# One load of wo split by rows: 96 rows in one DMA, 32 rows in four DMAs of eight

## The chip, the core and the metric

The kernel runs on one core of one Trainium2 chip. A core has TensorE (PE, matrix multiplies), VectorE (DVE), ScalarE (ACT), GpSimd (POOL) and SyncE (SP), which work side by side and wait for one another through semaphores. Data comes from the large memory (HBM) into the on-chip memory of 128 partitions, one row of a tile in each, by 16 DMA engines. A DMA instruction is issued on an engine's queue, here nearly always SP's; its rows are dealt to DMA engines, each of which moves its share packet by packet and then adds to the DMA's semaphore. The load counts as landed when the last of them has done so.

The metric is the device time of one execution in microseconds (us).

## The reference

One decode step of a gated mix of two layers, all in bf16, for four batches of one token with 512 features. Cut to what matters:

```python
# A: attention over the last 4096 of 16384 cached positions
q = (x @ wq)                      # 512 -> 32 heads of 128
k, v = last 4096 rows of the caches, 8 kv heads, each for 4 query heads
p = softmax(q k^T * 128 ** -0.5)
a = (p v) @ wo                    # 4096 -> 512
# B: gated linear unit
b = (relu(x @ W_gate) * (x @ W_up)) @ W_down     # 512 -> 1792 -> 512
g = sigmoid(sum(x * gate_w))
out = g * a + (1 - g) * b
```

The caches make up 64 of the 81 MB that are read; wo is 4 MB (4096 x 512).

## The kernel before

**Sets.** The work on the caches is cut into eight sets (NSET): one batch and four of the eight kv heads each. A set loads 4 MB of keys (`load_k`, L158) and 4 MB of values (`load_v`, L162), each as one DMA of 128 rows of 32 KB, into two buffers used in turn. PE turns the keys over (`kt`, L249), ACT and DVE copy them back, PE makes the scores (`scores`), DVE and ACT the softmax (`maximum`, `exponent`, `turn`), PE the product with the values (`values`, L328), and `combine` (L345) puts the heads' outputs, divided by their sums and weighted by g, into the tile oq.

**Order of the work.** The program is written out by hand. `Program` holds a list per engine, in the order in which `P.op` and `P.dma` are called; names stand for semaphore values, and an instruction waits for the names it lists. Every DMA has a semaphore of its own. `emit` (L59) writes one wait instruction for each semaphore that is needed and not yet seen by that engine.

**Loads.** All large loads go through SP's queue in one order: keys 0, wq, then keys and values by turns, W_gate and W_up (into the buffer that keys 6 have left), values 7, W_down, and last wo. SP waits before an issue only for the buffer to be free. wo goes into Wbig, where wq was, and so waits for Q, the last use of wq, which has long passed by then.

**wo.** Partition p of Wbig holds rows 32p to 32p + 31 of wo one behind another, 32 x 512 numbers, 32 KB. The load is cut by these 32 blocks at `WO_CUTS = (0, 16, 28, 32)` into three DMAs of all 128 partitions, with 16, 12 and 4 KB in each partition (L181 to L183). Sixteen DMA engines have eight partitions each.

**The end.** The last values and `combine(7)` are followed by W_down's 56 matmuls (L444), which start the sum in a PSUM bank AB, and wo's 128 (L452), four for each of the 32 blocks, which add to it. A wo matmul uses all 128 partitions of its block, so the 64 of the first piece can begin only when every row of it has landed:

```python
        for k in range(len(WO_CUTS) - 1):
            for i in range(WO_CUTS[k], WO_CUTS[k + 1]):
                ...
                        ("ACC",) if last else None, [("WO", k), ("OQ", NSET - 1)])
```

Then DVE copies AB (L456), PE turns it over (L459), DVE copies it again (L460) and SP stores it (L461).

Of the kernel before, what the change touches and what calls it, by code (L numbers as in the profile page):

```python
# [19 lines left out]
NSET = 8  # L20
# [9 lines left out]
WO_CUTS = (0, 16, 28, 32)  # L30
# [49 lines left out]
def bass_gated_mix__sliding_block_cached__glu_gated_reglu__decode_kernel(  # L80
# [13 lines left out]
    with ExitStack() as ctx:  # L94
        def sb(name, shape, dt):
            return ctx.enter_context(nc.sbuf_tensor(name, shape, dt))
# [3 lines left out]
        Wbig = sb("Wbig", [128, 16384], BF16)  # L100
# [47 lines left out]
        P = Program()  # L148
# [29 lines left out]
        P.dma("sp", lambda e: e.dma_start(Vsb[:, 0, 0:NFT * 512], B_W_down.rearrange("(p i) w -> p (i w)", p=128)),  # L178
              ("WD",), [("PV", NSET - 2, 3)])
        wo_src = A_wo.rearrange("(p i) w -> p (i w)", p=128)  # L180
        for k in range(len(WO_CUTS) - 1):  # L181
            lo, hi = 512 * WO_CUTS[k], 512 * WO_CUTS[k + 1]
            P.dma("sp", lambda e, lo=lo, hi=hi: e.dma_start(Wbig[:, lo:hi], wo_src[:, lo:hi]), ("WO", k), [("Q",)])  # L183


        P.op("pool", lambda e: e.memset(ones[:, :], 1.0), ("ONES",))
# [261 lines left out]
        for k in range(len(WO_CUTS) - 1):  # L448
            for i in range(WO_CUTS[k], WO_CUTS[k + 1]):
                for cb in range(4):  # L450
                    last = i == 31 and cb == 3
                    P.op("pe", lambda e, i=i, cb=cb, last=last: e.matmul(  # L452
                        AB[:, 4 * cb:4 * cb + 4], Wo3[:, i, cb * 128:(cb + 1) * 128], oq3[:, :, i],
                        start=False, stop=last, skip_group_check=True),
                        ("ACC",) if last else None, [("WO", k), ("OQ", NSET - 1)])
        P.op("dve", lambda e: e.tensor_copy(outT[:, :].rearrange("p (b c) -> p c b", c=4),  # L456
                                            AB[:, 0:16].rearrange("p (c b) -> p c b", c=4)), ("OUTT",), [("ACC",)])
        otb = SCB[1][:].bitcast(BF16)
# [54 lines left out]
```

## Time and profile before

| | |
|---|---|
| median of three runs | 199.39 us (199.17 to 199.5) |
| the profiled execution's own time | 199.14 us |
| its span, first to last instruction | 197.4 us |
| mean granted TensorE clock | 0.843 |
| read from HBM | 81.01 MB, 410 GB/s over the span |
| wo's three loads: issued at | 168.31, 168.75 and about 169.2 us |
| wo's three loads: time from issue to landing | 20.9, 24.1 and 24.9 us |
| W_down's matmuls (L444) | from 188.02, 1.65 us |
| wo's matmuls (L452) | from 189.53, 1.85 us, and from 192.94, 1.87 us |
| the output's store issued (L461) | 195.65 us |

The profile is one execution on the chip. Times are in us from the start of the span. The page gives busy time by engine, then slices of the span, DMA queues, the chain of work that ended last, and the costliest groups of instructions; in such a group the form is line, engine, operation, result <- operands, how often, and at the end the idle time before it with what ended it. Loads are listed with their size in KB and the median time from issue to landing. "SPq" is SP's own instruction stream, where the DMAs are issued.

### The profile page before, as it was taken

Reading aid. Unit: us, or ns where it says so; the run is one execution under the profiler, and the core shown is the slowest. Engines: PE = TensorE matmul, PEld = TensorE weight load, DVE = VectorE, ACT = ScalarE, POOL = GpSimd, SP = SyncE. Lnnn points to the kernel's source line nnn. Section 1 sums busy time; section 2 is a strip of 40 time slices with the busy share of each in tenths; the row PEclk is TensorE's granted clock in tenths of the full one; section 3 lists DMA queues with packets and bytes.
Section 4 is the critical chain, followed back from the end, with each engine's and each line's share of the span. In section 5 each row is a group of like instructions: output and inputs, shape, how many; then the busy total and the mean of one; then the engine's idle time right before and its main releaser. Section 6 shows DMA issues by size and latency. Waiting matters only on the chain.

```text
span 197.4 us, 4201 instructions
## 1 busy us (share of the span) xinstructions
PE 144.9 (73%) x1859; PEld 111.4 (56%) x1859; DVE 102.5 (52%) x277; ACT 91.6 (46%) x108; POOL 6.3 (3%) x31
## 2 busy tenths in 40 slices
PE   0139975989399929993999498839981999259874
PEld 0038842956287527753875386438641875259673
DVE  0105428395559457844684578437843694641110
ACT  2008800896097419740965198318830974400000
POOL 7500000000000000000000000000000000000000
PEclk9999965599979996997599789987999799955555
DMA  5999999999999999999999999999999999999970
GB/s 213 425 425 432 432 461 468 418 438 420 422 425 425 422 425 427 422 438 428 432 451 428 418 451 430 432 425 422 432 428 425 425 395 433 449 424 406 432 332 30
DMA packets 3371, 81.27 MB, mean 412 GB/s; under 512 B 405, under 2 KB 410, under 8 KB 538
## 3 DMA queue, kind: packets, MB, share of 16 engines
q1 hardware_dynamic: 3344, 81.01, 95.9%
q8 instruction: 14, 0.23, 0.5%
q14 instruction: 3, 0.02, 0.0%
q10 hardware_dynamic: 10, 0.01, 0.0%
HBM read 81.01 MB, written 0.00 MB: 410 GB/s over the span
## 4 chain that ended last, share of the span: by engine, by line
DMA 64%; PE 21%; ACT 6%; DVE 5%; SPq 1%; issue 1%
DMA Ksb<-in_A_k_cache_dram 52%; PE bank L260 13%; DMA Wbig<-in_A_wo_dram 12%; ACT Ksb L265 5%; PE bank L281 4%; DVE Ksb L267 3%; PE bank L337 2%; ACT sc L318 2%; DVE pT L325 1%; PE bank L350 1%; PE bank L452 1%; DVE sc L289 1%; SPq L159 0%; SPq L169 0%; SPq L183 0%
## 5 line engine op out<-in xcount | busy, mean ns | idle before, releaser
L260 PE MATMUL bank<-identf,Ksb 128*128 128x128 f32 x512 | 82.8, 319 | 32.1 <-DMA Ksb<-in_A_k_cache_dram 29.3
L265 ACT ACTIVATE Ksb<-bank 128x1024 bf16<-128x1024 bf16 x72 | 71.0, 1023 | 70.8 <-PE bank L260 70.5
L260 PEld LDWEIGHTS bank<-identf,Ksb 128*128 128x128 f32 x512 | 68.4, 164 | 46.8 <-DMA Ksb<-in_A_k_cache_dram 32.0
L267 DVE COPY Ksb<-bank 128x1024 bf16<-128x1024 bf16 x56 | 38.2, 686 | 47.4 <-PE bank L260 46.3
L289 DVE CUSTOM_DVE_ANT_0 sc<-bank,mask 128x512 bf16<-128x512 f32 x32 | 22.0, 687 | 11.3 <-PE bank L281 11.1
L281 PE MATMUL bank<-Ksb,QS 128*32 128x512 bf16 x256 | 21.2, 420 | 3.0 <-DVE Ksb L267 1.6
L325 DVE STREAM_TRANSPOSE pT<-sc 128x1024 bf16<-128x1024 bf16 x16 | 19.7, 1237 | 2.9 <-ACT sc L318 2.8
L337 PE MATMUL bank<-Vsb,pT 128*32 128x256 bf16 x512 | 20.8, 291 | 0.0
L318 ACT ACTIVATE sc<-sc,negmax 128x1024 bf16<-128x1024 bf16 x16 | 18.3, 1144 | 4.8 <-DVE negmax L310 4.7
L337 PEld LDWEIGHTS bank<-Vsb,pT 128*32 128x32 bf16 x512 | 12.8, 101 | 6.5 <-issue 2.4
L350 PEld LDWEIGHTS bank<-osb,Wsel 128*64 128x64 f32 x128 | 8.8, 148 | 4.6 <-issue 2.6
L281 PEld LDWEIGHTS bank<-Ksb,QS 128*32 128x32 bf16 x256 | 4.5, 100 | 11.3 <-DVE Ksb L267 4.1
L385 PE MATMUL bank<-xT,Ksb 128*128 128x4 bf16 x112 | 6.9, 199 | 5.3 <-DVE oq L358 5.3
L350 PE MATMUL bank<-osb,Wsel 128*64 128x32 f32 x128 | 9.7, 233 | 1.2 <-DVE mq L296 0.7
L385 PEld LDWEIGHTS bank<-xT,Ksb 128*128 128x128 bf16 x112 | 6.8, 162 | 5.3 <-issue 5.3
L310 DVE TENSOR_SCALAR negmax<-mall 32x1 f32<-32x1 f32 x32 | 4.6, 144 | 1.0
L296 DVE TENSOR_REDUCE mq<-mx 32x1 f32<-32x4 f32 x32 | 4.6, 143 | 0.8
L452 PE MATMUL bank<-oq,Wbig 128*128 128x4 bf16 x128 | 3.7, 168 | 1.6 <-DMA Wbig<-in_A_wo_dram 1.6
L342 DVE COPY osb<-bank 128x256 f32<-128x256 f32 x8 | 3.4, 420 | 2.8 <-PE bank L337 2.8
L227 PE MATMUL bank<-ident,xsb 5*128 5x5 bf16 x4 | 0.3, 167 | 5.8 <-POOL m L203 5.8
L452 PEld LDWEIGHTS bank<-oq,Wbig 128*128 128x128 bf16 x128 | 3.6, 103 | 1.6 <-DMA Wbig<-in_A_wo_dram 1.6
L389 DVE TENSOR_SCALAR gtmp<-bank 128x56 f32<-128x56 f32 x1 | 0.2, 217 | 7.0 <-PE bank L385 7.0
(55 smaller groups left out, 44.9 us busy)
## 6 DMA issues: line engine op xcount, KB each, us to landing
Ksb<-in_A_k_cache_dram SPq DMA_DIRECT2D x8, 4096.0 KB, 23.1
Vsb<-in_A_v_cache_dram SPq DMA_DIRECT2D x8, 4096.0 KB, 32.5
Wbig<-in_A_wq_dram SPq DMA_DIRECT2D x1, 4096.0 KB, 21.4
Wbig<-in_A_wo_dram SPq DMA_DIRECT2D x1, 2048.0 KB, 20.9
Ksb<-in_B_W_gate_dram SPq DMA_DIRECT2D x1, 1792.0 KB, 19.0
Ksb<-in_B_W_up_dram SPq DMA_DIRECT2D x1, 1792.0 KB, 22.9
Vsb<-in_B_W_down_dram SPq DMA_DIRECT2D x1, 1792.0 KB, 16.4
Wbig<-in_A_wo_dram SPq DMA_DIRECT2D x1, 1536.0 KB, 24.1
```

The costliest lines, as they stand in the source:

```text
L260: P.op("pe", lambda e, bk=bk, cc=cc, c=c, s=s: e.transpose(bk[:, cc * 128:(cc + 1) * 128], kw[:, c * 128:(c + 1) * 128], identf[:, :]), (" ...
L265: P.op("act", lambda e: e.activation(dst, bk[:, :].bitcast(BF16), ACTF.Copy), ("KTC", s, i), [("KT", s, i)])
L267: P.op("dve", lambda e: e.tensor_copy(dst, bk[:, :].bitcast(BF16)), ("KTC", s, i), [("KT", s, i)])
L281: P.op("pe", lambda e, a=a, h=h: e.matmul(bk[32 * a:32 * a + 32, 0:512], QS[:, NSET * h + s, :], k4[:, 16 * bank:16 * bank + 16, 32 * a:32 ...
L289: P.op("dve", lambda e: e.tensor_tensor_reduce(sc[:, s % 2, bank * 512:(bank + 1) * 512], bk[:, :], mask[:, :], 1.0, LOWEST, ALU.add, ALU.max,
L296: P.op("dve", lambda e, a=a: e.tensor_reduce(mq[:, a:a + 1], mx[32 * a:32 * a + 32, par, :], AXIS.X, ALU.max), ("MAXQ", s, a), [("SCC", s, ...
L318: P.op("act", lambda e: e.activation(sc[:, par, k * PW:(k + 1) * PW], sc[:, par, k * PW:(k + 1) * PW], ACTF.Exp, bias=negmax[:, par:par + ...
L325: P.op("dve", lambda e: e.transpose(pT[:, par, k * PW:(k + 1) * PW], sc[:, par, k * PW:(k + 1) * PW]), ("PTT", s, k), [("EXP", s, k), ("PV ...
L337: P.op("pe", lambda e, c=c, g=g, col=col: e.matmul(OB[32 * g:32 * g + 32, 0:256], pT[:, par, col:col + 32], v3[:, 16 * k + c, :], start=(k ...
L350: P.op("pe", lambda e, k=k, lo=lo: e.matmul(FB[r, 256:288], Wsel[:, lo:lo + 64], osb[:, par, 32 * k:32 * k + 32], start=(k == 0), stop=(k ...
L385: P.op("pe", lambda e, W=W, i=i, t=t, col=col: e.matmul(FB[:, col:col + 4], W[:, t, i:i + NFT * 127 + 1:NFT], xT[:, t * 8:t * 8 + 4], star ...
L452: P.op("pe", lambda e, i=i, cb=cb, last=last: e.matmul(AB[:, 4 * cb:4 * cb + 4], Wo3[:, i, cb * 128:(cb + 1) * 128], oq3[:, :, i], start=F ...
```

## The change

The first of wo's three loads is issued as five DMAs in place of one: rows 0 to 95 in one DMA, and rows 96 to 127 in four of eight rows each. The columns (16 KB in each partition) stay as they are, and so do the second and third loads, so that wo takes seven DMAs instead of three. The matmuls of the first piece wait for the five semaphores of its parts. No other instruction is changed; SP has four DMA instructions more, PE four waits more.

```diff
         wo_src = A_wo.rearrange("(p i) w -> p (i w)", p=128)
-        for k in range(len(WO_CUTS) - 1):
+        def load_wo(k, r0, r1):
             lo, hi = 512 * WO_CUTS[k], 512 * WO_CUTS[k + 1]
-            P.dma("sp", lambda e, lo=lo, hi=hi: e.dma_start(Wbig[:, lo:hi], wo_src[:, lo:hi]), ("WO", k), [("Q",)])
+            P.dma("sp", lambda e: e.dma_start(Wbig[r0:r1, lo:hi], wo_src[r0:r1, lo:hi]), ("WO", k, r0), [("Q",)])
+
+        load_wo(0, 0, 96)
+        for r0 in range(96, 128, 8):
+            load_wo(0, r0, r0 + 8)
+        for k in range(1, len(WO_CUTS) - 1):
+            load_wo(k, 0, 128)
+        wo_parts = [[("WO", 0, r0) for r0 in (0, 96, 104, 112, 120)]] + [[("WO", k, 0)] for k in range(1, len(WO_CUTS) - 1)]
...
                         start=False, stop=last, skip_group_check=True),
-                        ("ACC",) if last else None, [("WO", k), ("OQ", NSET - 1)])
+                        ("ACC",) if last else None, wo_parts[k] + [("OQ", NSET - 1)])
```

## The prediction

> **What bounds the kernel now.** I read the page first: engine shares, DMA line and queues.
>
> ```profile
> PE 144.9 (73%) x1859; PEld 111.4 (56%) x1859; DVE 102.5 (52%) x277; ACT 91.6 (46%) x108; POOL 6.3 (3%) x31
> ...
> DMA  5999999999999999999999999999999999999970
> ...
> q1 hardware_dynamic: 3344, 81.01, 95.9%
> q8 instruction: 14, 0.23, 0.5%
> q14 instruction: 3, 0.02, 0.0%
> ```
>
> No compute engine is full; the DMA engines are, from the second slice to the 38th. SP's queue (q1) moves 81.01 MB and fills 95.9% of the time of 16 engines. The kernel is as long as its loads, so what matters is how evenly the last ones end. Note also the 14 small packets of q8 (16 KB each) and the three of q14 (8 KB): they fetch instructions and use the same engines.
>
> Then the chain that ended last, at its end, and the timeline of the same stretch:
>
> ```profile
> 168.31 0.43 SPq L183
> 168.75 0.04 issue
> 168.79 24.11 DMA Wbig<-in_A_wo_dram
> 192.89 0.04 issue
> 192.94 1.88 PE bank L452 x64
> 194.85 0.21 DVE outT L456
> ```
>
> ```profile
> 189.53 1.85 PE L452 MATMUL bank<-oq,Wbig 128*128 128x4 bf16 x64
> 192.94 1.87 PE L452 MATMUL bank<-oq,Wbig 128*128 128x4 bf16 x64 [1.56 <-DMA Wbig<-in_A_wo_dram]
> ```
>
> PE uses wo's first piece from 189.53 to 191.38, idles 1.56 us, and goes on when the second piece has landed, at 192.89. From there to the end of the span is 4.5 us of dependent work. The first piece (landed 189.2) does not hold PE: at 189.53 PE had just finished w_down. The third (194.2) is in before PE comes to it, 48 matmuls after 192.94, at about 194.35. So the time to watch is the landing of the second piece on its slowest engine. Sizes and landings:
>
> ```profile
> Wbig<-in_A_wo_dram SPq DMA_DIRECT2D x1, 2048.0 KB, 20.9
> Vsb<-in_B_W_down_dram SPq DMA_DIRECT2D x1, 1792.0 KB, 16.4
> Wbig<-in_A_wo_dram SPq DMA_DIRECT2D x1, 1536.0 KB, 24.1
> Wbig<-in_A_wo_dram SPq DMA_DIRECT2D x1, 512.0 KB, 24.9
> xsb<-in_A_x_dram ACTq DMA_DIRECT2D x1, 4.0 KB
> ```
>
> Last, the trace's records of single DMA packets (start, length, size, queue; not the engine). On one engine a packet starts about 4 ns before the one ahead ends, so 16 chains can be followed through, and each ends its share of a load with a 4-byte semaphore packet. These 16 per load show the skew. For the second piece (clock of the span): six engines at 189.66 to 189.95, one at 190.46, one at 191.81, three at 191.16 to 191.42, and five at 192.82 to 192.90. The cause is in the chains. Each q8 fetch costs its engine about 1.55 us (1.0 to 1.1 us itself, 0.5 us more on the next packet) and the 14 go round the same eight engines: five had two before the end, three had one. The other eight have none; on one of them two q14 fetches fell (0.94 + 0.99 us: the one at 191.81), on another one (0.68: at 190.46). So there is a slow eight, ending at 192.90, and a fast eight, ending at 191.81 with seven of them by 190.46.
>
> **The change, part by part.** *Removed:* one load of 128 rows of 16 KB; each engine had eight rows of 611 ns: 4.89 us. *Added:* a load of 96 rows, six an engine (3.67 us), and four loads of eight rows. x's load of four rows left four semaphore packets, four engines with one row each; so I take eight rows as eight engines with a row each, the same eight every time. Those get 6 + 4 = 10 rows, the other eight 6. If a row costs 611 ns wherever it goes, the ten-row engines end 1.22 us later, the six-row engines 1.22 us earlier. Each of four further semaphore packets takes 6 ns: 0.02. Thus +1.25 and -1.22.
>
> *Which eight.* The trace does not number its engines. gate_w's load (one row, one engine) sat in a chain without q8 fetches, by its place among the 32 KB packets, though another chain lies 3 ns off. [...] I take them to be the fast eight.
>
> *What a row costs when eight neighbouring rows are written at once.* This decides, and the trace has no large case. Below: 0.61 us a load of eight rows, the price of one row by itself. Above: 4.89 us, since in every large load here one engine alone fills its eight rows and no such set was filled faster. Between lies the only load in which several engines write neighbouring rows: x's. Its four packets of 1 KB took 93, 51, 44 and 44 ns and 92 ns from first start to last end: 4 KB in 92 ns, 44.5 GB/s for four engines, where one 16 KB packet alone runs at 16384/611 = 26.8. At that rate 128 KB takes 2.94 us if the eight rows share it, 1.47 us if each four have it to themselves. [...] I take the middle, 2.2 us.
>
> [...]
>
> *Sum.* A fast engine now needs 6 x 0.61 + 4 x 2.2 = 12.5 us for the first piece instead of 4.89, 7.6 more. The six at up to 189.95 end the second piece at about 197.55. The late one (191.81) would come to 199.4, but it is 1.9 us behind, nearly one load, so its last row has no neighbours: 0.61 instead of 2.2, giving 197.8. The slow eight end earlier and no longer matter. The landing moves from 192.90 to 197.8: +4.9. The profiled execution took 199.14 (span 197.4 and 1.7 around it): 204.0. The median shown is 199.39, 0.25 above, so as a median 204.3.
>
> *Costed at nothing.* Four more issues on SP, 0.43 us each (L183): the second and third pieces are issued 1.7 us later, at about 170.5, while their first packet starts at 186.0; behind the 15 us backlog of loads that is free. If it ran dry, 1.7 us would show. Behind them SP only waits for the output (25.9 us idle), so it has time. Four more semaphore waits on PE before the first wo matmul: by the 0.04 us between steps in the chain at most 0.16 us, under PE's wait for the second piece (1.56 us); without that they would count whole. PE's 1.85 us of work on the first piece stays hidden: on each engine the second piece ends 3.7 us after the first (eight packets of 12 KB at 0.46). The 96-row load deals rows six to an engine, so engines may write in each other's old groups: from nothing to what the same sharing costs, at most 6 x (1.1 - 0.61) = 3 us, if two meet on most rows; I take nothing and keep 3 us for the upper end.
>
> **Rivals.** *Same: rows cost 0.61 anywhere.* Then the fast engine with two q14 fetches sets the landing: 191.81 + 1.25 = 193.06, +0.16 us: 199.3, as a median 199.55. For it: in the large loads every engine keeps 26.8 GB/s with all 16 at work, so nothing common to them binds. Against it: no load here lets engines share a group of rows.
>
> *Faster: rows cost 0.61 and the late engine is not among the eight, or its q14 fetches fall elsewhere.* The landing is then set by the six-row engines at 192.90 - 1.22 = 191.68 and the engine with one q14 fetch at 190.46 + 1.25 = 191.71: -1.19 us, 197.95, as a median 198.2. It decides once the slowest of the loaded eight stands below 191.65 now; seven stand at 190.46 or less. Against it: the late chain took no q8 fetch, so it belongs with the fast ones.
>
> *Slightly slower: rows cost 0.61, but one of the five late engines is among the eight*, since engine numbers are not known: 192.90 + 1.25, +1.25 us, as a median 200.6. For it: the packets that start first in the run, eight at once and eight 0.6 us later, mix chains with and without fetches.
>
> *The change does not spread at all:* each eight-row load is filled at one engine's rate, 4.89 us. Lockstep would give +18.3 us on the fast engines, about 215; x's overlapping packets speak against it. I fold it into the upper tail.
>
> **How the numbers follow.** Sharing (the forecast) 0.60, of which 0.05 lies above 208; slow engine loaded 0.10; same 0.16; faster 0.14. Slower is 0.60 + 0.10 = 0.70, same 0.16, faster 0.14; 0.2% is 0.4 us, about what a measurement of this kernel can tell. Alone, the forecast runs from 1.47 us a load (6 x 0.61 + 4 x 1.47 = 9.5, +4.7: 194.65 for the six, near +1.8 us, and up to +3.5 with the late one whole: 201 to 203) to 2.94 (+10.5: 200.5 for the six, +7.6: 207), and 208 with part of the 3 us. The whole range, with the three others: 198.2 to 208, which leaves out half of the faster case and the upper tail, 0.12, and little else.
>
> **What would show it.** In the profile after: SP with seven issues of wo at L183 (0.43 each); the second piece landing near 198 instead of 192.9, PE's wait before its second 64 matmuls over 3 us, the 38th and 39th of the 40 DMA slices about half busy, since eight engines run alone there; the 16 KB packets of the last 32 rows at 1.5 to 3 us instead of 0.61. If those packets stay at 0.61, the forecast is wrong and one of the first three rivals holds; which one, the semaphore packets of the second piece tell (193.06, 191.7 or 194.15). If the six-row packets are also stretched, the re-dealt 96 rows are the cause.

## The result, and the profile after

The changed kernel takes 211.31 us (median of 4 runs, 208.47 to 211.52), the kernel before 199.38: ratio 1.0567, 95% interval 1.0477 to 1.0657. It is 12 us slower. Slower was forecast, but by 4.9 us and at most 208.

The chain that ended last, at its end, in the changed kernel:

```profile
168.74 0.43 SPq L183
...
170.63 34.53 DMA Wbig<-in_A_wo_dram
205.16 0.05 issue
205.21 1.88 PE bank L459 x64
207.09 0.02 issue
207.11 0.20 DVE outT L463
```

The second piece of wo lands at 205.16 instead of 192.89: +12.3 us, which is all that the profiled execution (211.38) lost. From there to the end (209.7) it is 4.5 us, as before. The timeline of the same stretch shows who waited. Before, W_down's matmuls (`w_down` from here on) began without a wait, and after:

```profile
188.02 1.65 PE L444 MATMUL bank<-hT,Vsb 128*128 128x4 bf16 x56
```

```profile
188.48 1.56 PE L451 MATMUL bank<-hT,Vsb 128*128 128x4 bf16 x56 [0.84 <-DMA Vsb<-in_B_W_down_dram]
201.83 1.85 PE L459 MATMUL bank<-oq,Wbig 128*128 128x4 bf16 x64 [11.79 <-DMA Wbig<-in_A_wo_dram]
205.21 1.87 PE L459 MATMUL bank<-oq,Wbig 128*128 128x4 bf16 x64 [1.52 <-DMA Wbig<-in_A_wo_dram]
```

Two things stand here that the prediction did not have. The first piece itself now keeps PE waiting 11.8 us. And w_down, which is queued *ahead* of everything that was changed and whose load is the same in both kernels, landed later, so that PE waited 0.8 us for it as well. In the lists of loads it took 20.1 us from issue to landing, before 16.4:

```profile
Vsb<-in_B_W_down_dram SPq DMA_DIRECT2D x1, 1792.0 KB, 20.1
```

Stretches of 5 us of both kernels, with the share of time that the DMA engines were busy and what they moved in GB/s (the last two columns; a packet counts whole in the stretch in which it starts). Before, where wo's last load lands at 194.2:

```profile
core 0: us, PE busy (x) PEld busy (x) DVE busy (x) ACT busy (x) POOL busy (x), PEclk, DMA share, GB/s
176.00:181.00 5.00, 5.00 (x86) 5.00 (x86) 0.00 (x0) 0.00 (x0) 0.00 (x0) 0.50 0.92 386
181.00:186.00 5.00, 4.47 (x80) 3.22 (x79) 1.08 (x4) 0.00 (x0) 0.00 (x0) 0.50 1.00 421
186.00:191.00 5.00, 5.00 (x129) 4.98 (x130) 0.65 (x3) 0.00 (x0) 0.00 (x0) 0.50 0.95 397
191.00:196.00 5.00, 2.52 (x80) 2.16 (x76) 0.41 (x2) 0.00 (x0) 0.00 (x0) 0.50 0.24 97
```

After:

```profile
176.00:181.00 5.00, 5.00 (x87) 5.00 (x86) 0.00 (x0) 0.00 (x0) 0.00 (x0) 0.50 0.95 394
181.00:186.00 5.00, 4.90 (x87) 3.71 (x86) 0.70 (x4) 0.00 (x0) 0.00 (x0) 0.50 1.04 214
186.00:191.00 5.00, 2.77 (x74) 2.60 (x74) 1.02 (x4) 0.00 (x0) 0.00 (x0) 0.84 1.04 194
191.00:196.00 5.00, 0.00 (x0) 0.00 (x0) 0.00 (x0) 0.00 (x0) 0.00 (x0) 0.50 0.99 177
196.00:201.00 5.00, 0.00 (x0) 0.00 (x0) 0.00 (x0) 0.00 (x0) 0.00 (x0) 0.50 0.87 220
```

From 181 on, all 16 engines are as busy as before and move half as much. That is not imbalance, where some engines would be done and idle; it is every engine at half speed for 20 us. In these 20 us 4.0 MB were moved, which at the 421 GB/s of before takes 9.6 us: 10.4 of the 12.3 us are here. The trace's records of single packets say the same: a 16 KB packet of the first piece took 614 ns before (median of 128), 1339 ns after, and the 12 KB packets of the second piece, whose load was not changed, 861 instead of 462. The slowing begins before any of the four small loads has moved a byte: the first 60 of the 16 KB packets, all of the 96-row load, already took 1234 ns (median).

### The profile page after: what moved, and what is told of

It is laid out like the page before. It is cut to its first block, busy times and chain, and to the rows that moved or that the text cites. A ratio compares the mean times of both kernels' runs of the same rounds, so it can differ in the third digit from the quotient of the medians.

```text
span 209.7 us, 4207 instructions
## 1 busy us (share of the span) xinstructions
PE 143.7 (69%) x1859; PEld 110.4 (53%) x1859; DVE 102.7 (49%) x277; ACT 91.5 (44%) x108; POOL 6.2 (3%) x31
## 4 chain that ended last, share of the span: by engine, by line
DMA 65%; PE 21%; ACT 6%; DVE 5%; SPq 2%; issue 1%
DMA Ksb<-in_A_k_cache_dram 48%; DMA Wbig<-in_A_wo_dram 16%; PE bank L267 13%; PE bank L288 4%; ACT Ksb L272 4%; DVE Ksb L274 3%; PE bank L344 2%; DVE pT L332 1%; ACT sc L325 1%; PE bank L357 1%; PE bank L459 1%; SPq L183 1%; ACT L325 1%; DVE sc L296 1%; SPq L159 0%
## 5 line engine op out<-in xcount | busy, mean ns | idle before, releaser
L459 PEld LDWEIGHTS bank<-oq,Wbig 128*128 128x128 bf16 x128 | 3.6, 103 | 13.5 <-issue 11.9
L357 PEld LDWEIGHTS bank<-osb,Wsel 128*64 128x64 f32 x128 | 8.1, 138 | 4.9 <-issue 2.9
L357 PE MATMUL bank<-osb,Wsel 128*64 128x32 f32 x128 | 8.9, 224 | 1.2 <-DVE mq L303 0.7
## 6 DMA issues: line engine op xcount, KB each, us to landing
Vsb<-in_B_W_down_dram SPq DMA_DIRECT2D x1, 1792.0 KB, 20.1
```

The source lines that it names most:

```text
L357: P.op("pe", lambda e, k=k, lo=lo: e.matmul(FB[r, 256:288], Wsel[:, lo:lo + 64], osb[:, par, 32 * k:32 * k + 32], start=(k == 0), stop=(k ...
L459: P.op("pe", lambda e, i=i, cb=cb, last=last: e.matmul(AB[:, 4 * cb:4 * cb + 4], Wo3[:, i, cb * 128:(cb + 1) * 128], oq3[:, :, i], start=F ...
```

## The experiments

Two theories. **Neighbours** (on record): only the loads of eight neighbouring rows are dear, for the engines that do them. **Groups** (formed on the result): the eight rows that one engine fills in a load of 128 rows are a group that takes no more than one engine's rate; whoever writes into another engine's group slows both. Which eight rows these are stands in no trace; the author took them to be four neighbours and the four 32 rows further on. What bears on it: beside one engine's single rows in 0-3 and 32-35 a load of 128 rows ran at 456 GB/s, beside those in 92-95 and 124-127 at 399, with two engines slowed and 14 not (m_pairs, in slices of 2.3 us). Below, "own rows" are an engine's group, "others' rows" the groups of other engines. The 96-row load, six rows to an engine, then breaks this order as the eight-row loads do.

**1. The price of a shape by itself** (m_shapes). Behind the output of the kernel before, fourteen loads, each alone:

```diff
         P.op("sp", None, None, [("OUT",)])
+        P.dma("sp", lambda e: e.dma_start(Wbig[0:128, :], wo_src[0:128, :]), ("T", 0), [("OUT",)])
+        P.dma("sp", lambda e: e.dma_start(Wbig[0:96, :], wo_src[0:96, :]), ("T", 1), [("T", 0)])
...
+        P.dma("sp", lambda e: e.dma_start(Wbig[96:104, :], wo_src[0:32:4, :]), ("T", 7), [("T", 6)])
+        P.dma("sp", lambda e: e.dma_start(Wbig[0:32:4, :], wo_src[96:104, :]), ("T", 8), [("T", 7)])
...
```

> The kernel before with fourteen more loads at its end, each alone (issued when the one ahead has landed), from wo into Wbig, whose contents are then no longer needed; the output is unchanged. Rows of 32 KB; a row by itself takes 1.21 us of packet time in the trace of before, and every load has a start and an end of some 1.5 to 2 us that is not packet time. Group theory: the eight rows that one engine fills in a load of 128 rows (four neighbours, and four more elsewhere) can together take no more than one engine's rate. Then packet time is 9.7 us for 128 rows, at least 9.7 for rows 0-95 and for rows 0-63, 4.9 for 32 rows, for 16 neighbours, for 8 neighbours and for 4 neighbours, and 1.2 for 8 or 4 rows that lie four apart; 2.4 for two neighbours. Spreading theory (rows cost the same everywhere): 9.7, 7.3, 4.9, 2.4, 1.2, 1.2 and 1.2 for 8 or 4 rows, near or apart. Two loads take neighbours on one side and rows four apart on the other: if it is the side written that shares, neighbours written cost 4.9 and neighbours only read 1.2; if it is the side read, the other way about.

What SP waited for each of them (us in total, times, longest). The load waited for stands one line above the one that waits: L464 waits for 128 rows, then come 96, 64, 32 and 16 rows, eight neighbours (L469), eight rows four apart (L470), neighbours written and rows apart read (L471), rows apart written and neighbours read (L472), four neighbours, four apart, two neighbours, one row (L476). The fourteenth, sixteen rows four apart in rows 0-63, took 4.3 us.

```profile
SPq L465 <- DMA Wbig<-in_A_wo_dram: 16.7, 1, 16.7
SPq L466 <- DMA Wbig<-in_A_wo_dram: 12.1, 1, 12.1
SPq L464 <- DMA Wbig<-in_A_wo_dram: 11.9, 1, 11.9
...
SPq L469 <- DMA Wbig<-in_A_wo_dram: 6.2, 1, 6.2
...
SPq L471 <- DMA Wbig<-in_A_wo_dram: 6.1, 1, 6.1
...
SPq L470 <- DMA Wbig<-in_A_wo_dram: 3.2, 1, 3.2
SPq L472 <- DMA Wbig<-in_A_wo_dram: 3.1, 1, 3.1
SPq L476 <- DMA Wbig<-in_A_wo_dram: 3.1, 1, 3.1
```

96 rows take 16.7 us, longer than 128 (11.9), and 64 rows as long as 128 (12.1). One row takes 3.1 us, 1.9 more than a packet of 32 KB takes in the kernel before (1.21). Eight rows that lie four apart cost no more than one row (3.2 against 3.1), eight neighbours twice that, and of the two mixed loads the one that *writes* neighbours is slow (6.1 against 3.1): the sharing is on the written side. Spreading falls. By packets, from the first start to the last end, 128 rows go at 384 GB/s, 96 at 202, 64 at 198 and 32 at 193. The group theory holds in kind; in size it gave 4.9 us of packet time for eight neighbours, and 4.5 with start-up was measured. For 96 rows it said only "at least 9.7", and 15.6 was measured. Which rows of a 96-row load fall to which engine stands in no trace; only the six rows to an engine do.

**2. The cut by rows without the imbalance** (t_96_32).

```diff
-        for r0 in range(96, 128, 8):
-            load_wo(0, r0, r0 + 8)
+        load_wo(0, 96, 128)
```

> Rows 0-95 in one load and rows 96-127 in one load of 32 rows (two rows an engine), so that all engines carry the same and only the cut by rows is left. The theory that came out of the result (the 96-row load itself is slow, since its rows are dealt to engines that share groups of rows): slower than before by 5 to 13 us, most of what the change lost. The theory on record (only eight neighbouring rows at a time are dear, the 96-row load costs nothing): 32 neighbours in a load of two rows an engine cost at most 2 x (2.2 - 0.61) = 3.2 us, and between 0 and 3 us slower.

207.22 us, ratio 1.0393 [1.0373, 1.0413]: 7.8 us slower than before. The neighbour theory's 0 to 3 us fall. In the same stretches:

```profile
181.00:186.00 5.00, 5.00 (x92) 3.87 (x90) 0.65 (x3) 0.00 (x0) 0.00 (x0) 0.50 1.12 230
186.00:191.00 5.00, 3.83 (x78) 3.57 (x74) 1.07 (x4) 0.00 (x0) 0.00 (x0) 0.50 0.96 196
```

Half the rate again, and here w_down too came 19.6 us after its issue instead of 16.4. No engine carries more than another. So the cut at row 96 alone costs about two thirds of what was lost (this kernel has a load of 32 neighbours in it as well, which the changed one has not).

**3. Eight rows four apart, with the 96-row load** (t_spread8).

```diff
-        for r0 in range(96, 128, 8):
-            load_wo(0, r0, r0 + 8)
+        for r0 in range(96, 100):
+            load_wo(0, r0, r0 + 29)
...
+            st = 4 if r1 - r0 == 29 else 1
+            P.dma("sp", lambda e: e.dma_start(Wbig[r0:r1:st, lo:hi], wo_src[r0:r1:st, lo:hi]), ("WO", k, r0), [("Q",)])
```

> The changed kernel with the four loads of eight rows taken four rows apart (96, 100, ... 124 and so on) in place of neighbours. Theory on record: without neighbours an eight-row load costs 0.61 us a row, and the time falls back to that of before (199.5) or near it. Group theory with a slow 96-row load: some 1 to 3 us better than the changed kernel, and still 205 to 210.

208.94 us (two runs near 207.5, two at 210.3 and 210.9), ratio 1.0476 [1.0391, 1.0561]. Undoing the neighbours wins back 2.4 us of 12 by the medians, but the intervals of the two kernels overlap, so a gain is not shown; the time is nowhere near 199.5. Neighbours are not the whole cause.

**4. Eight neighbours without the 96-row load** (t_cols_next). The first piece is cut by columns: 12 blocks for all rows, 4 blocks in sixteen loads of eight rows. Each engine has the bytes that the change gives it.

```diff
+        load_wo(("WO", 0, 0), slice(0, 128), 0, 12)
+        for n in range(16):
+            load_wo(("WO", 0, n + 1), slice(8 * n, 8 * n + 8), 12, 16)
```

> No 96-row load: 12 of the first piece's 16 blocks for all 128 rows in one load, and the last 4 blocks (4 KB a row) in sixteen loads of eight neighbouring rows. The bytes per engine are those of the change (32 KB more for eight engines, 32 KB less for the others). Theory on record: a 4 KB row with neighbours costs 2.2/4 = 0.55 us, sixteen of them 8.8 us instead of 2.5, so as slow as forecast for the change, about 204. Group theory: the four neighbours share one engine's rate, 16 x 0.6 us = 9.7 instead of 2.5, less for engines that are out of step: second piece landing 2 to 4 us later, 201.5 to 204. If rows cost the same everywhere: 199.5. If small loads have a cost of their own, it shows here four times over, above 206.

203.36 us, ratio 1.0182 [1.0147, 1.0217]: +4.0 us. That is near the 4.9 of the prediction, but by luck, and not by its mechanism: a 4 KB row of the sixteen loads took 0.24 us (median; 0.30 at most) where the prediction's price gives 0.55, and the 12 KB packets of the two loads of 128 rows, which the price leaves alone, were stretched as well (median 0.60 us instead of 0.46). The next run takes the neighbours away, and most of the loss stays. Small loads have no large cost of their own: four times as many as in the change, and a third of its loss.

**5. The same bytes, eight rows four apart** (t_cols_apart).

```diff
-            load_wo(("WO", 0, n + 1), slice(8 * n, 8 * n + 8), 12, 16)
+            load_wo(("WO", 0, n + 1), slice(32 * (n // 4) + n % 4, 32 * (n // 4) + n % 4 + 29, 4), 12, 16)
```

> As the form with 12 blocks in one load and sixteen loads of eight neighbouring rows (203.36), but the eight rows of a load lie four apart. No two of the eight engines then write into one group; each shares only with the late engine whose group it is in, and only for rows 64-127. Bytes per engine are again those of the change. Group theory: the bytes into each group are those of before, so nothing can be won, and up to 1.3 us is lost: 199.4 to 201. Engine theory (only neighbours in one load matter, a balance of engines counts): 198.2 to 199.6.

202.56 us (201.84 to 203.48; with neighbours 201.90 to 203.49), ratio 1.0161 [1.0121, 1.0201]. Without neighbours 3.2 of the 4.0 us stay, and the two runs are not told apart. The engine theory (198.2 to 199.6) falls: a balance of bytes over engines is worth nothing when it is bought by writing into other engines' groups. But 3.2 us is more than the 0 to 1.3 us that sharing in pairs could cost by the author's estimate. The next two say where it is.

**6 and 7. The same eight engines, own rows and others' rows** (t_more_low, t_more_high). Eight extra loads of eight rows, 4 KB a row, between the first and the second piece, into a tile that nothing reads.

```diff
+        def load_more():
+            for n in range(8):
+                rows = slice(0 + 32 * (n // 4) + n % 4, 0 + 32 * (n // 4) + n % 4 + 29, 4)   # 64 + ... in t_more_high
+                P.dma("sp", lambda e, rows=rows: e.dma_start(spare[rows, :], wo_src[rows, 0:2048]), ("MORE", n), [("Q",)])
```

> The kernel before with eight extra loads between wo's first and second piece, of eight rows four apart each, 4 KB a row, rows 0-63 only, into a tile that nothing reads. Eight engines get 32 KB more (1.25 us, as in the change), no engine gets less, and each of the eight writes where it writes in a load of 128 rows. It asks which eight engines the loads of eight rows use. If they are the eight without instruction fetches: second piece at 191.81 + 1.25 = 193.06, 199.3 to 199.6, no change that can be told. If late ones are among them: 192.90 + 1.25, 200.5 to 200.8. If small loads are dear in themselves: above 201.

> The same with rows 64-127: the same eight engines, the same extra bytes, but written into the rows that the other eight engines fill. Group theory: each extra 4 KB row takes its time from the late engine whose group it is, which is delayed by up to the whole 1.2 us: second piece at up to 194.1, 0.5 to 1.3 us slower than with rows 0-63 (200.0 to 200.8). If only engines count: as with rows 0-63. Were the late engines those that fill rows 0-63, it would be the other way about.

Own rows: 199.52 us, ratio 1.0017 [1.0000, 1.0033], as the prediction's reading of the chains says (+0.16 us for a fast eight that gets 1.25 us more). Eight of the ten runs took 199.35 to 199.55. So in these the loads of eight rows ran on engines that were not late, and these do fill rows 0-63. The other two took 200.66 and 200.72, the 200.5 to 200.8 that was expected if late engines are among the eight, and the trace kept is of 200.72: the engine that ends the second piece last (its 12 KB packets run from 190.31 to 193.97, the load lands at 194.45) moved rows of the extra loads just before. So which engines are late is not the same in every execution.

Others' rows: 202.16 us, ratio 1.0148 [1.0128, 1.0169], 2.6 us more for the same bytes in loads of the same shape. The stretches of the two kernels, rows 0-63 first:

```profile
181.00:186.00 5.00, 5.00 (x94) 4.22 (x95) 0.65 (x3) 0.00 (x0) 0.00 (x0) 0.50 0.98 417
186.00:191.00 5.00, 4.47 (x102) 4.03 (x95) 1.07 (x4) 0.00 (x0) 0.00 (x0) 0.50 1.00 415
```

and rows 64-127:

```profile
181.00:186.00 5.00, 5.00 (x91) 3.83 (x89) 0.65 (x3) 0.00 (x0) 0.00 (x0) 0.50 1.01 421
186.00:191.00 5.00, 3.78 (x78) 3.57 (x74) 1.07 (x4) 0.00 (x0) 0.00 (x0) 0.50 0.99 230
```

For 5 us everything runs at 230 instead of 415 GB/s. By the packet records, at 190.2 us all 16 engines are at half speed (nine 12 KB packets at 889 to 948 ns, four 16 KB packets at 1195 to 1231) though only three of them still write into others' rows. The group theory in its local form falls here: the stall reaches engines that share nothing.

**8. Less for the late engines** (t_leave): the column form with the last eight loads, those of rows 64-127, taken out.

> A quarter of the first piece is left out for rows 64-127: 12 of 16 blocks are loaded for all rows, the last 4 blocks only for rows 0-63, in eight loads of eight rows four apart (the products with the rows left out use what lies there). Seven eighths of the piece's bytes. If the late engines are the other eight, filling rows 64-127, they end 1.22 us earlier: second piece at 191.8, bound by the engine at 191.81, 1.0 to 1.2 us faster, 198.2 to 198.4. If they fill rows 0-63, nothing is gained: 199.4 or above.

198.80 us, ratio 0.9973 [0.9954, 0.9992], 0.6 us faster where 1.0 to 1.2 was expected. Seven of the ten runs took 198.18 to 198.96, three 199.51 to 199.70. The trace kept is of 199.65, and there too the engine that ends the second piece last moved rows of the small loads just before: in such an execution the engines that were relieved are not the late ones. In the other seven, by their times, the late engines are the ones that fill rows 64-127, and relief helps; the changed kernel's wish was sound, but the gain within reach is this small.

**9. How far the stall reaches** (m_pairs, m_dose, m_kinds). Again steps behind the output, each alone; in most of them a few engines are kept busy with single rows while a load of 128 rows runs on the others, as in

```diff
+        P.dma("sp", lambda e: e.dma_start(Ksb[64:69:4, 0, :], wo_src[64:69:4, :]), ("T", 9), [("T", 0), ...])
...
+        P.dma("sp", lambda e: e.dma_start(Wbig[0:128, :], wo_src[0:128, :]), ("T", 17), [])
```

> The kernel before with seven steps at its end, rows of 32 KB, each step issued when the one ahead has landed; the output is unchanged. Steps 1 to 3: eight rows four apart among rows 0-31 (where the eight engines write in a load of 128 rows), eight rows four apart among rows 64-95 (where the other eight write, idle here), eight rows eight apart among rows 0-63 (two rows to a group). Step 4: 128 rows. Steps 5 and 6: eight loads of one row, which go to one engine, and behind them 128 rows, so that the other engines work on the 128 rows while the one is still busy with single rows; in step 5 these are rows 0-3 and 32-35, in step 6 rows 92-95 and 124-127, another engine's. Step 7: one row (64), then 128 rows. Local sharing: steps 1 and 2 take the same; in step 6 only the engine that owns rows 92-95 and 124-127 is slowed, the packets of the others stay at 1.21 us, as in step 5. Sharing that stops everyone: in step 6 the packets of all engines are stretched towards 2.4 us while the single rows are written, and step 6 takes 2 to 5 us longer than step 5. If an engine is slow wherever it writes outside its own rows, step 2 is slower than step 1.

> The kernel before with five steps at its end, rows of 32 KB, the output unchanged. In each step eight loads go to the same one, two, four or eight engines, one row each, four rows apart, written into rows of the other eight engines (64-127), and a load of 128 rows follows; the fifth step has eight engines and their own rows (0-63). The single pair seen before slowed only the two engines that met, and with eight pairs at once in the whole kernel all sixteen engines ran at half rate, also those with nothing to share. Purely local sharing: in the steps with one, two and four pairs 2, 4 and 8 engines have packets near 2.4 us and the rest stay at 1.21; with eight pairs all sixteen are at 2.4 only while their own pair meets. Sharing that spreads: with four or eight pairs engines outside the pairs are stretched as well. The fifth step: all at 1.21 throughout.

> The kernel before with four steps at its end, rows of 32 KB, the output unchanged; in each, small loads keep one or two engines busy with other engines' rows and a load of 128 rows follows. Before, one engine in another's rows slowed only these two, two engines in two others' rows slowed all sixteen. Step 1: one engine in the rows 4-7 and 36-39. Step 2: two engines, one in those rows, one in the rows 8-11 and 40-43. Step 3: two engines in one other's rows (64-67, 96-99), two neighbours to a load. Step 4: the same, rows 32 apart. If what counts is that two different engines are disturbed: step 1 slows two engines, step 2 all sixteen, steps 3 and 4 only three. If two disturbers are enough: steps 2, 3 and 4 slow all sixteen. If it takes the other half of the rows (64-127): step 2 slows four engines at most.

m_pairs: eight rows four apart go as fast into rows 64-95 as into rows 0-31 (packets 2.07 and 2.18 us from first to last); eight rows eight apart in rows 0-63, two to a group, take 2.56. One engine in another's rows: the two that meet have 32 KB packets of 2.40 to 2.57 us, the other 14 keep 1.213. Two writers thus get 2 x 32768 / 2.42 us = 27.1 GB/s together, what one gets alone (32768 / 1.213 us, 27.0). "Sharing that stops everyone" falls for one pair.

m_dose, from inside the steps with one, two and eight engines in others' rows, and eight in their own:

```profile
206.00:211.00 5.00, 0.00 (x0) 0.00 (x0) 0.00 (x0) 0.00 (x0) 0.00 (x0) 0.50 0.97 393
236.00:243.00 7.00, 0.00 (x0) 0.00 (x0) 0.00 (x0) 0.00 (x0) 0.00 (x0) 0.50 1.01 211
...
292.00:297.00 5.00, 0.00 (x0) 0.00 (x0) 0.00 (x0) 0.00 (x0) 0.00 (x0) 0.50 0.92 203
324.00:327.00 3.00, 0.00 (x0) 0.00 (x0) 0.00 (x0) 0.00 (x0) 0.00 (x0) 0.50 0.86 371
```

One pair: 393 GB/s. Two pairs: 211, and all 16 engines at 2.48 to 2.61 us a packet. Four pairs: all 16 at 2.55. Eight pairs: 203, hardly worse than two. As soon as the last of the single rows is written, all are back at 1.21. So two engines that write into the rows of two others halve the whole core's loads. The changed kernel shows the same half rate from 181 to 201 us; that its 96-row load makes such meetings is inferred, as which rows an engine fills there was not seen.

m_kinds: two engines in *one* other's rows (neighbours or 32 apart) put the three that meet at 4.0 us and the other 13 at 1.51, about 306 GB/s in all by these times (13 x 32768 / 1.51 + 3 x 32768 / 4.0 us); it is a stall that spreads with its size, neither "only three" nor the full half for all. One engine in the rows next to its own slows two (393 GB/s inside the step), as in rows 64-127. The step with two engines each in the next one's rows slowed only two (410 GB/s), but there the owner of the first rows was itself the second writer, so only one group was disturbed; whether it takes the upper half of the rows stays open.

**10. wo in four pieces** (t_cuts). PE's last wait suggests smaller pieces at the end.

```diff
-WO_CUTS = (0, 16, 28, 32)
+WO_CUTS = (0, 16, 24, 30, 32)
```

> The kernel before with wo in four pieces of all 128 rows, 16, 8, 6 and 2 blocks, in place of three of 16, 12 and 4. Every engine keeps its bytes and its rows. From the profile of before: the second piece then lands 4 x 0.46/3 x 2 = 1.2 us earlier (191.7) and PE has only the last 2 blocks left (8 matmuls, 0.23 us) when the last piece lands at 194.2, so the sum is done at about 194.5 instead of 194.8: 0.3 us, 0.15%, faster, or not to be told from no change.

199.11 us, ratio 0.9987 [0.9978, 0.9996]: 0.13% faster where 0.15% was expected, and the fastest of the kernels here that compute everything. Every load has 128 rows. The way it was expected to come about is not shown: in the trace (of 199.27 us) PE does its last 32 matmuls, not 8, from 193.83, and DVE's copy begins at 194.89, before 194.85.

## Why the prediction was wrong

- *What bounds the kernel.* Right: the landing of the second piece set the end, 4.5 us from there on, before and after.
- *Which eight engines, and that they are the fast ones.* The author's assumption, which no run shows directly; by the times of the runs it was right in most executions: eight of ten with own rows, seven of ten with the others relieved (6, 8). In the rest a late engine was among the eight, the rival "slightly slower" with its 200.6 (200.66 and 200.72 in 6). The changed kernel's trace seems to be of this kind: as far as its chains can be followed, the engine that ends the second piece last began its six rows at 187.3, 6.7 us after the first engine, and had four more. What this adds there was not measured.
- *The direction, and sharing as the cause.* Right.
- *What a row costs among eight neighbours, 2.2 us for 16 KB.* The author's choice between 1.47 and 2.94, and too high: alone, neighbours of 32 KB took 3.0 to 3.8 us, so 1.5 to 1.9 for 16 KB, and in the changed kernel no row of the first piece took over 1.89, though all were stretched by then. That neighbours without the cut at row 96 cost 4.0 us (4) where the sum had 4.9 does not bear it out, since 3.2 of it stay without neighbours (5).
- **The step that failed is the term put at nothing: "The 96-row load deals rows six to an engine, so engines may write in each other's old groups ... I take nothing and keep 3 us for the upper end."** It is the largest term: instead of 0, the cut at row 96, with the other 32 rows spread evenly, costs 7.8 us (2), and a 96-row load alone runs at 202 GB/s instead of 384 (1). The bound of 3 us was wrong because it let sharing cost only the rows that meet: 6 x 0.49. Measured, two meetings are enough to halve all 16 engines (211 GB/s instead of the 393 with one, 9), those included that are still busy with w_down (20.1 us to landing instead of 16.4) or already with the second piece. The prediction's own last sign came: the packets of the six-row load were stretched, to 1.23 us before any other part of the change had moved.
- *"Slow eight end earlier and no longer matter."* Wrong for the same reason: their packets were stretched like the others' (over all engines 1339 ns for 16 KB instead of 614, 861 for 12 KB instead of 462).
- *PE's wait for the second piece over 3 us, the 38th and 39th slices half busy.* PE waited 11.8 us before the first piece and 1.5 before the second: the prediction had the first piece hidden. Of the slices the 39th was half busy, but the 38th was full, at 201 GB/s instead of 432: the engines were busy, and slow.
- *Four more issues on SP at nothing.* Right: the second piece was issued by 171, and its first packet moved only at about 188 (186 before).
- *Rivals.* The three with rows at 0.61 us anywhere fall with the packet times. The rival in which each load fills at one engine's rate (215) was nearer in time, for a reason that does not hold: eight neighbours alone took 6.2 us, twice one row, not eight times.

That 7.8 us (cut at row 96 with 32 even rows) and 4.0 us (small loads of neighbours, no cut) make up the 11.9 of the change is a coincidence: both act by the same stall, and the small loads of the second cover all rows. What the change loses beyond the 7.8 us, by its small loads or by late engines among the ten-row ones, is not taken apart.

## What to carry to other kernels

In a load of all 128 rows, as these runs fit together, each DMA engine fills rows that no other one fills (384 GB/s alone). A load of 96 rows (202 GB/s alone) or of eight neighbouring rows (6.2 us, four apart 3.2) breaks this order, and beside a running 128-row load it slowed that one too: with the 96 rows even w_down, queued ahead, took 20.1 us instead of 16.4, and with the neighbours 12 KB packets took 0.60 us instead of 0.46 (4). A load of 64 rows ran at the same half rate alone (198 GB/s). To move work between DMA engines, cut by columns and keep every engine in its own rows (for eight engines, rows four apart among rows 0-63: 199.52 us for the extra loads, against 202.16 in rows 64-127); handing the rows that land late to other engines gained nothing (202.56 us, before 199.39). When a cost is unknown because a step touches what others use, bound it by what all of them would lose, not by the rows that meet.

## What the runs showed that was not expected

- 96 rows took longer to load than 128: 16.7 against 11.9 us.
- One engine writing in another's rows: two engines at half speed. Two engines in two others' rows: all sixteen, 211 GB/s. Three in one group: 4.0 us a packet for these three, 1.51 for the rest. Why a stall of two pairs reaches engines with nothing to share was not found.
- Two neighbouring rows alone, on two engines, hardly shared (4.0 us against 3.1 for one row, 2.27 against 2.13 by packets), while four neighbours took 6.2. The group theory's one rate does not give this; for loads so short it stays open.
- An instruction fetch of 16 KB costs its DMA engine about 1.55 us, where 16 KB of data take 0.61. In the kernel before the fetches went round eight engines, which lag by up to 3 us for it. Which engines are late is not the same in every execution: one program was up to 1.2 us slower in two of ten (6), and in the one that was traced a late engine had the extra rows.
